# Reordering experts, attention pairs and the first pairs of a fused attention, expert and feed-forward kernel

## Chip, core and metric

One core of one Trainium2 chip runs the whole program in one launch. The metric is the device time of one execution in microseconds (us).

## What is computed

Inputs are `q`, `k`, `v` of shape (4, 8, 576, 64), embeddings of 8 experts with weights `w1` (8, 512, 1024) and `w2` (8, 1024, 512), and a feed-forward layer `w_in` (512, 2048), `w_out` (2048, 512).

```
q_rot, k_rot = rotate(q), rotate(k)
attn = softmax(scale * q_rot @ k_rot.T)            # per batch and head
x = (attn @ v) laid out as 2304 tokens x 512
idx = argmax over 8 experts of cosine(x, expert_emb) / tau;  gate = its softmax probability
y[token] = gate * relu(x @ w1[idx]) @ w2[idx]      # one expert for each token
h = y @ w_in;  g = h if h > 0 else exp(h) - 1
out = g @ w_out
```

With these inputs four experts get nearly all tokens: experts 1, 5, 6 and 2 get 709, 691, 722 and 173, experts 0 and 4 get 6 and 3, and two get none.

## The kernel before

**Attention.** The 32 heads run as 16 pairs p of two heads. A pair has nine score tiles. First come plain scores `sc` (PE, L327), whose row maxima `sc_max` (DVE, L337) are turned by `m_turn` (two PE matmuls, L347 and L348, a copy to fp16 on ACT, L350, and two small DMAs that ACT issues, L352 and L353) into a row of the stacked operand. Then come the scores again, less the maximum, `st` (PE, L363 and L364, exp on ACT, L365; no `st` tile of a pair may start before that row has landed). `p_lo` (L377, DVE or POOL) makes the low half of a split number, and `pv` (PE, L401) multiplies by v, followed by the row sums (L409). `o_out` (ACT) takes the result out, `o_turn` (PE, L427) transposes it, and `epi` (DVE, L442 to L451) divides by the sums. Operands of `sc` and `st` are made ahead: `load` (SP), `rope` (DVE or POOL), `hi` (ACT, L286) and `lo` (DVE, L290), and `stack`, six SP DMAs (L296 to L300) that copy the split halves into a buffer D4. Numbers are kept as a high and a low fp16 part, so most products take three matmuls.

**Routing and experts.** After each batch's four pairs `r_hi`, `r_lo`, `r_turn_pe`, `r_logits`, `r_acc` give logits, `r_pick`, `r_rank` and `r_slot` give every token a place, and `r_put` writes it out. The experts then run in visits j of up to 128 rows of one expert: visits 0 to 4 from the first three batches, before the last routing is known, and up to 20 more from tables (`tab_head`, `tab_visits`) that list experts in an order. In that order the early expert comes first, and then by size with small experts put between large ones. A visit is `mm1` (PE, L1057 to L1059), `relu` (L1069 ACT, L1070 DVE), `mm2` (PE, L1094 to L1096) and `y_out`. Where the expert changes (`chg`), `w_load` fetches its weights on SP as eight DMAs of 512 KB (L1009, L1012) and `w_conv` splits them (L1029 ACT, L1031 DVE); else a branch, `when` (L993), skips them. The tables give visits 0 to 5 to expert 1, 6 to expert 0, 7 to 12 to 5, 13 to 4, 14 to 19 to 6, and 20 and 21 to expert 2; three visits stay unused.

**Feed-forward.** Nine groups of 256 rows, `ff1` (L1139 to L1141), `elu`, `ff2` (L1191 to L1193), `fold`, store. Its weights are made into a form of 24 bits in two parts by `widen` on DVE, ACT and POOL during the earlier stages, column by column (32 columns), in weight buffers that `w_load` also uses: a buffer index b of 11 serves `w_load` until its column's due time.

**Order.** All tasks are listed with a hand-written time (`add(t, f, ...)`, corrected by the table OFF), sorted, and issued in that order to each engine's in-order queue. Pair p begins at 9p, the experts at ZV = 144.6; a visit is 2 units of ZU = 2.7.

Of the kernel before, what the change touches and what calls it, by code (L numbers as in the profile page):

```python
# [45 lines left out]
def kernel(ctx: ExitStack, tc: tile.TileContext, qk, vp, cs, cf, tid, emb, tau, w1, w2, wi, wo, out, tag=None):  # L46
# [174 lines left out]
    def emb_norm(i):  # L221
# [121 lines left out]
    def m_turn(p):  # L343
# [8 lines left out]
        nc.scalar.dma_start(out=d[64:65, 0, 1], in_=ms[0:5])  # L352
        nc.scalar.dma_start(out=d[0:1, 1, 1], in_=ms[5:10])  # L353
# [24 lines left out]

    def pv(p, kt):
# [309 lines left out]
    def tab_head():  # L689
# [113 lines left out]
    add(-22.0, c_prep)  # L803

    VT = (4.6, 6.2, 7.7, 9.6, 11.4)
    UT = [t - VT[0] for t in VT]
    for p in range(NP):
# [3 lines left out]
        add(z - 36 if p else z - 38.5, load, p, 1)  # L811
        for i in range(6):
            add(g - 33.3 + 1.5 * i if p else g - (33, 32.9, 32.85, 33, 32.8, 32.5)[i], rope, p, i)
        for f, i, t in ((hi, 0, -26.1), (lo, 0, -25), (hi, 1, -20.6), (lo, 1, -19.4)) if p else ((hi, 0, -25.6), (lo, 0, -24.6), (hi, 1, -24.5), (lo, 1, -23.6)):
            add(g + t, f, p, i)
        add(g - (19.3 if p else 23.5), stack, p)
        u, w = (z - 13.45, 1) if p else (z - 19, .3)
# [564 lines left out]
```

## Time and profile before

| | us |
|---|---|
| median of 3 runs | 1009.29 (1006.53 to 1009.57) |
| the profiled execution | 1010.61 |
| its span | 1008.8 |
| PE busy | 901.2 (89%) |
| DVE, POOL, ACT busy | 669.7, 546.3, 502.3 |
| PE idle before matmuls of L327 | 37.0 |

PE is the busiest engine and mostly full. What the span loses is idle time of PE in a few stretches and the time in which PE was granted half its clock (mean 0.948 of full). The stretches are the head (to 44 us), the 16 pairs (to 361), the passage from the last pair to the experts (to 385), the experts (to 631) and the feed-forward groups.

### The profile page before, as it was taken

How to read it: one execution, taken by the hardware profiler on the slowest of the kernel's cores; microseconds unless marked ns; L12 is line 12 of the kernel's file. 1: busy time of each engine (PE TensorE's matmuls, PEld its weight loads, DVE VectorE, ACT ScalarE, POOL GpSimd, SP SyncE). 2: the span in 40 equal slices, each digit the busy share in tenths (PEclk: the TensorE clock that was granted, in tenths of full speed). 3: DMA queues.
4: the chain of work that ended last, by engine and by line, in shares of the span. 5: the costliest groups of instructions: out<-in, count | busy, mean ns of one | idle time of the engine just before them, and what ended most of it. 6: DMA issues, size and time to landing. Idle time of an engine off the chain costs nothing. (4 is left out here: it accounts for less than half of the span.)

```text
span 1008.8 us, 24500 instructions
## 1 busy us (share of the span) xinstructions
PE 901.2 (89%) x9398; PEld 655.4 (65%) x9398; DVE 669.7 (66%) x1070; ACT 502.3 (50%) x858; POOL 546.3 (54%) x652
## 2 busy tenths in 40 slices
PE   3398999998989779999999876998999999999994
PEld 0154555554445467776776652887888888888884
DVE  8556757867868547778786874775665565664651
ACT  1244464464464633565665444645555555555540
POOL 6475565685643203424428544366776765766640
PEclk8588999999999979999999987999999999999998
DMA  7554465584463844997997674401201202201000
GB/s 261 152 166 107 129 156 136 142 200 127 133 144 104 251 85 144 328 249 200 260 304 175 192 203 92 123 2 43 64 22 43 64 22 43 65 22 44 22 22 21
DMA packets 127094, 127.65 MB, mean 127 GB/s; under 512 B 71272, under 2 KB 105064, under 8 KB 126960
## 3 DMA queue, kind: packets, MB, share of 16 engines
q1 hardware_dynamic: 118000, 97.68, 37.5%
q0 software_dynamic: 8352, 27.62, 8.5%
q8 instruction: 76, 1.25, 0.5%
q10 hardware_dynamic: 608, 0.63, 0.2%
q14 instruction: 58, 0.48, 0.2%
HBM read 79.15 MB, written 17.35 MB: 96 GB/s over the span
## 5 line engine op out<-in xcount | busy, mean ns | idle before, releaser
L1139 PE MATMUL banks<-arena 128*128 128x256 f16 x576 | 157.1, 273 | 2.4 <-ACT arena L1154 2.4
L1141 PE MATMUL banks<-arena 128*128 128x256 f16 x576 | 157.1, 273 | 0.0
L1140 PE MATMUL banks<-arena 128*128 128x256 f16 x576 | 157.1, 273 | 0.0
L365 ACT ACTIVATE arena<-banks 128x576 f32<-128x576 f32 x144 | 89.8, 652 | 125.8 <-PE banks L364 108.5
L1191 PE MATMUL banks<-arena 128*128 128x256 f16 x504 | 138.2, 274 | 5.5 <-DVE arena L1206 5.5
L1174 DVE TENSOR_TENSOR arena<-arena 128x896 f16<-128x896 f32 x72 | 79.9, 1110 | 89.0 <-ACT arena L1170 84.0
L1192 PE MATMUL banks<-arena 128*128 128x256 f16 x504 | 138.2, 274 | 0.0
L1193 PE MATMUL banks<-arena 128*128 128x256 f16 x504 | 138.2, 274 | 0.0
L1170 ACT ACTIVATE arena<-arena 128x896 f16<-128x896 f32 x71 | 67.5, 951 | 122.7 <-POOL arena L1167 121.4
L337 DVE TENSOR_REDUCE MH<-banks 128x1 f16<-128x576 f32 x144 | 103.2, 751 | 34.1 <-PE banks L327 32.3
L1059 PE MATMUL banks<-arena 128*128 128x128 f16 x704 | 122.4, 222 | 1.5 <-DVE arena L1031 1.5
L1057 PE MATMUL banks<-arena 128*128 128x128 f16 x704 | 122.5, 222 | 0.0
L1058 PE MATMUL banks<-arena 128*128 128x128 f16 x704 | 122.5, 222 | 0.0
L1164 POOL TENSOR_TENSOR arena<-arena 128x256 f32<-128x256 f32 x67 | 54.1, 808 | 91.4 <-DVE arena L1161 91.4
L983 POOL TENSOR_TENSOR arena<-arena 128x896 f16<-128x896 f32 (+1 forms) x32 | 51.6, 1611 | 86.1 <-ACT arena L981 65.7
L401 PE MATMUL banks<-arena 128*64 128x256 f32 (+9 forms) x768 | 90.9, 362 | 4.6 <-DVE arena L377 4.6
L363 PE MATMUL banks<-arena 128*128 128x288 f16 (+1 forms) x320 | 79.5, 299 | 3.5 <-DVE l L523 2.2
L327 PE MATMUL banks<-arena 64*128 64x288 f16 (+1 forms) x320 | 48.5, 313 | 37.0 <-DVE MH L337 16.2
L1095 PE MATMUL banks<-arena 128*128 128x512 f16 x176 | 70.2, 399 | 10.2 <-DVEq L993 9.6
L364 PE MATMUL banks<-arena 128*128 128x288 f16 (+1 forms) x320 | 78.5, 294 | 0.0
L1094 PE MATMUL banks<-arena 128*128 128x512 f16 x176 | 69.8, 396 | 6.0 <-ACT arena L1069 4.4
L377 POOL TENSOR_TENSOR arena<-arena 128x576 f16<-128x576 f32 x26 | 30.2, 1162 | 79.8 <-ACT arena L365 79.8
(238 smaller groups left out, 2285.2 us busy)
## 6 DMA issues: line engine op xcount, KB each, us to landing
arena<-in_w_dram SPq DMA_DIRECT2D x48, 512.0 KB
arena<-in_qk_dram SPq DMA_DIRECT2D x30, 576.0 KB
arena<-in_wo_dram SPq DMA_DIRECT2D x32, 256.0 KB
arena<-in_wi_dram SPq DMA_DIRECT2D x16, 512.0 KB
arena<-arena SPq DMA_DIRECT2D x32, 216.0 KB
yreg<-arena POOLq DMA_DIRECT2D x25, 260.0 KB, 4.0
arena<-arena SPq DMA_DIRECT2D x32, 144.0 KB
arena<-in_vp_dram SPq DMA_DIRECT2D x16, 256.0 KB
```

The source lines that it names most:

```text
L337: nc.vector.tensor_reduce(out=MH1[p % 2][:, c:c + 1], in_=t[:, :, 0:288], op=ALU.max, axis=AX.XY, negate=True)
L365: nc.scalar.activation(P32[:, (9 * p + i) % RP].rearrange("p (c n) -> p c n", c=2), t[:, :, 0:288], AF.Exp, scale=2.0)
L401: nc.tensor.matmul(o[64 * e:64 * e + 64, c, 0:QC[c].stop - QC[c].start], lhsT=w, rhs=x[:, QC[c]], start=first and n == 0, stop=end and n = ...
L1057: nc.tensor.matmul(o[:, fc], lhsT=w[:, 0, a], rhs=x[:, k], start=k == 0, stop=False)
L1058: nc.tensor.matmul(o[:, fc], lhsT=w[:, 0, a], rhs=x[:, 4 + k], start=False, stop=False)
L1059: nc.tensor.matmul(o[:, fc], lhsT=w[:, 1, a], rhs=x[:, k], start=False, stop=k == 3)
L1139: nc.tensor.matmul(o[:, v], lhsT=wih[k][:, f0:f0 + 128], rhs=z[:, :, k], start=k == 0, stop=False)
L1140: nc.tensor.matmul(o[:, v], lhsT=wih[k][:, f0:f0 + 128], rhs=z[:, :, 4 + k], start=False, stop=False)
L1141: nc.tensor.matmul(o[:, v], lhsT=wil[k][:, f0:f0 + 128], rhs=z[:, :, k], start=False, stop=k == 3)
L1191: nc.tensor.matmul(y, lhsT=a, rhs=b, start=u + f + n == 0, stop=False)
L1192: nc.tensor.matmul(y, lhsT=a, rhs=w[:, 1, WB[i - 1]], start=False, stop=False)
L1193: nc.tensor.matmul(y, lhsT=q[:, 1, f, GB[i - 1]], rhs=b, start=False, stop=u + f == 4 and n == len(m) - 1)
```

## The change

It has four parts. (1) **Head.** Pair 0's fourth rope goes from POOL to DVE; the 512-column cast of `c_prep` goes to ACT (`c_copy`), and the rest of `c_prep` later; `emb_norm` moves behind the first score tiles, with two operations from DVE to ACT; `warm` has 10 matmuls, not 13; `stack(0)` is issued half by SP and half by ACT, the pieces that `sc` reads first; pair 1's `hi`, `lo` and `stack` move to an own buffer and earlier; `sc(1)` moves from ahead of `st(0, 0)` to between the tiles of `st(0)`, and `sc(2)` later. (2) **Pairs.** The row sums become a task of their own, `ps`, 0.02 to 0.8 behind their `pv`; `m_turn` moves 0.78 later, and for p > 0 its DMAs go from ACT to SP; `o_out` moves 0.5 and `o_turn` 0.35 later. (3) **Passage.** `w_conv(0, ·)`: two in the middle of pair 15, two at its end; `p_lo`, `o_out`, `o_turn` of pair 15 earlier; its `r_turn_pe`, `r_logits` later, among the first visits' matmuls, as the tables. (4) **Experts.** The expert of rank 2 in the order gets 7 added, and so becomes the last: visits 14 and 15 go to expert 2, and 16 to 21 to expert 6; the `widen` columns 16 to 29 of `w_out` mostly move behind visit 17 (26 and 27 earlier), at 0.85 units a column in place of 0.9, so that four more weight buffers serve `w_load` until then.

```diff
+    def c_copy():
+        nc.scalar.copy(c16, cft[:, 0:512])
...
         elif i == 4:
-            nc.vector.tensor_scalar(et, et, n8[:, 1:2], 32.0, op0=ALU.mult, op1=ALU.mult)
+            nc.scalar.activation(et, et, AF.Copy, scale=n8[:, 1:2])
...
     def stack(p):
         h, t = hlt.pop(p), D4[p % 4]
+        if p == 0:
+            for e, eng in ((0, nc.sync), (1, nc.scalar)):
+                a, o = slice(64 * e, 64 * e + 64), slice(64 - 64 * e, 128 - 64 * e)
+                eng.dma_start(out=t[a, e, 0:3:2, 0:576], in_=h[a, 0:3:2])
+                eng.dma_start(out=t[a, e, 1, 0:576], in_=h[a, 1])
+                eng.dma_start(out=t[o, e, 0:3:2, 0:576], in_=h[a, 0:4:3])
+                eng.dma_start(out=t[a, e, 3, 0:576], in_=h[a, 2])
+            return
...
         d = D4[p % 4]
-        nc.scalar.dma_start(out=d[64:65, 0, 1], in_=ms[0:5])
-        nc.scalar.dma_start(out=d[0:1, 1, 1], in_=ms[5:10])
+        eng = nc.sync if p else nc.scalar
+        eng.dma_start(out=d[64:65, 0, 1], in_=ms[0:5])
+        eng.dma_start(out=d[0:1, 1, 1], in_=ms[5:10])
...
+        po[p, kt] = ones
+
+    def ps(p, kt):
+        o, ones, end = obank, po.pop((p, kt)), kt == PVO[-1]
...
+        pl_ = tbv(864, 8)
+        nc.vector.tensor_scalar(pl_, rk, 2.0, 7.0, op0=ALU.is_equal, op1=ALU.mult)
+        yield
         nc.vector.tensor_tensor(rk, rk, ps_, op=ALU.add)
+        yield
+        nc.vector.tensor_tensor(rk, rk, pl_, op=ALU.add)
...
-        add((-24.2, -24, -21.2, -21.1, -21, -20.9, -20.8)[i], emb_norm, i)
-    add(4, emb_turn)
-    add(-25.5, warm, OFF.get('WN', 13))
+        add((3.5, 5.5, 9.2, 9.3, 10.4, 11.4, 12.4)[i], emb_norm, i)
+    add(17.4, emb_turn)
+    add(-25.5, warm, 10)
...
-        u, w = (z - 13.45, 1) if p else (z - 19, .3)
+        ht = {0: (-25.6, -24.6, -24.5, -23.6, -23.5), 1: (-18.2, -18, -16.8, -16.5, -16.4), 2: (-8.2, -7, .4, .8, .9), 3: (4.8, 5.2, 6.4, 7.6, 7.7)}
...
+        u, w = {0: (-19, .3), 1: (.6, .6), 2: (6.2, .95)}.get(p, (z - 13.45, 1))
...
-        add(u + w * (UT[4] + (2.9 if p else 1.3)), m_turn, p)
+        add(u + w * (UT[4] + (3.68 if p else 1.3)), m_turn, p)
...
-                add(z + n + 1.8, p_lo, p, i)
-        for kt, t in zip(PVO, VT if p < NP - 1 else (4.6, 5.9, 7.5, 9.3, 10.4)):
+                add(z + n + (1.8 if p < NP - 1 else .9 if i < 8 else .4), p_lo, p, i)
+        for kt, t in zip(PVO, VT if p < NP - 1 else (4.6, 5.9, 7.5, 8.7, 9.4)):
             add(z + t, pv, p, kt)
-        add(z + (11.8 if p < NP - 1 else 10.6), o_out, p)
-        e = z + (14.7 if p < NP - 1 else 11.4)
+            add(z + t + (.01 if p == NP - 1 else ST5[kt]), ps, p, kt)
+        add(z + (12.3 if p < NP - 1 else 9.45), o_out, p)
+        e = z + (15.05 if p < NP - 1 else 10)
...
-            q, dt, sp = (y + 1, .2, .1) if last else (y + 10.2, .25, .5) if b == B - 2 else (y + 15.5, .5, 2.2)
+            q, dt, sp = (y + 6.8, .2, .1) if last else (y + 10.2, .25, .5) if b == B - 2 else (y + 15.5, .5, 2.2)
...
-    WT |= dict(zip(range(16, 30), (23.6, 30, 30.9, 31.8, 32.7, 33.6, 34.5, 35.4, 36.3, 37.2, 38, 39.3, 40.2, 42.2)))
+    WT |= dict(zip((26, 27, 16, 17, 18, 19, 20, 21, 22, 23, 24, 25, 28, 29), (23.2, 29, 34, 34.85, 35.7, 36.55, 37.4, 38.25, 39.1, 39.95, 40.8, 41.65, 42.5, 43.35)))
...
-            cv.append((use[j - 1, 2 * q + 1] + .01 if j else (-1.8, -1.1, -.4, .3)[q], j, q))
+            cv.append((use[j - 1, 2 * q + 1] + .01 if j else (-2.44, -1.85, .0075, .28)[q], j, q))
...
-        t0 = max(t0, free[b], {0: -4.8, 1: 0}.get(j, 1 if j < NE else 5.4)) + .001
+        t0 = max(t0, free[b], {0: -4.8, 1: 0}.get(j, 1 if j < NE else 5.8)) + .001
```

Line numbers shift: L290 becomes L293, L337 becomes L348, L350, L352 and L353 become L361, L364 and L365, L365 becomes L377, L1009 and L1012 become L1038 and L1041.

**DVE in the head.** The rows from the cast to the first maxima of pair 0 (L337 of before, L348 of after), before:

```order
L178 CAST c_67<-cft 128x512
L179 MEMSET tot 128x8
L180 RECIPROCAL rtau<-taut 128x1
L181 MEMSET chg 128x25
L182 TENSOR_SCALAR rtau<-rtau 128x1
L281 TENSOR_TENSOR arena<-arena 128x576
L227 TENSOR_SCALAR n_100<-n_100 8x1
L229 RECIPROCAL n_100<-n_100 8x1
L231 TENSOR_SCALAR arena<-arena,n_100 8x512
L233 CAST arena<-arena 8x512
L235 TENSOR_TENSOR arena<-arena 8x512
L337 TENSOR_REDUCE MH_92<-banks 128x1 x4
```

And after, from the third operation of the fourth rope (L284) on; L293 is `lo`:

```order
L284 TENSOR_TENSOR arena<-arena 128x576
L293 TENSOR_TENSOR arena<-arena 128x576 x2
L280 TENSOR_TENSOR arena<-arena 128x576
L284 TENSOR_TENSOR arena<-arena 128x576
L348 TENSOR_REDUCE MH_92<-banks 128x1 x4
L293 TENSOR_TENSOR arena<-arena 128x576
L348 TENSOR_REDUCE MH_92<-banks 128x1 x5
L352 COPY MH_94<-MH_92 128x1
```

The cast (L178), `c_prep` (L179 to L182) and `emb_norm` (L227 to L235) no longer stand ahead of the maxima; two rope operations (L280, L284) do.

**ACT in an ordinary pair.** From `o_out` of one pair (L415, L416) over exps (L365) and `m_turn` (L350 to L353) to `hi` (L286) and `r_hi` (L462), before:

```order
L415 COPY arena<-banks 128x384
L416 COPY arena<-banks 128x512
L365 ACTIVATE arena<-banks 128x576 x3
L350 CAST ms<-banks 10x128
L352 DMA arena<-ms 1x5x128
L353 DMA arena<-ms 1x5x128
L365 ACTIVATE arena<-banks 128x576
L286 ACTIVATE arena<-arena 128x576
L462 ACTIVATE arena<-arena 128x5x128
```

And after, where `o_out` is L433, the exp L377 and the copy of `m_turn` L361:

```order
L433 COPY arena<-banks 128x384
L434 COPY arena<-banks 128x512
L377 ACTIVATE arena<-banks 128x576 x3
L361 CAST ms<-banks 10x128
L289 ACTIVATE arena<-arena 128x576
L480 ACTIVATE arena<-arena 128x5x128
```

The two DMA issues have left ACT.

**SP in the passage.** From the reading of the first expert's number (`eidx`) over its weights, before:

```order
L1002 TENSOR_LOAD eidx
L1002 ISA x2
L1009 ISA
L1009 DMA arena<-in_w_dram 128x4x256
L1009 ISA
L1009 DMA arena<-in_w_dram 128x4x256
L1009 ISA
L1009 DMA arena<-in_w_dram 128x4x256
L1009 ISA
L1009 DMA arena<-in_w_dram 128x4x256
L1012 ISA
L1012 DMA arena<-in_w_dram 128x2x512
```

And after; L364 and L365 are `m_turn(15)`, which stood on ACT before:

```order
L1038 ISA
L1038 DMA arena<-in_w_dram 128x4x256
L1038 ISA
L1038 DMA arena<-in_w_dram 128x4x256
L1038 ISA
L1038 DMA arena<-in_w_dram 128x4x256
L1038 ISA
L1038 DMA arena<-in_w_dram 128x4x256
L364 DMA arena<-ms 1x5x128
L365 DMA arena<-ms 1x5x128
L1041 ISA
L1041 DMA arena<-in_w_dram 128x2x512
```

The last pair's two small DMAs now stand behind four weight loads in SP's queue and ahead of the other four.

## Rows read from the trace of the kernel before

**Rows 1.** waits of PE by what released them: us in total, times, longest.

```profile
PE banks L1095 <- DVEq L993: 9.6, 3, 4.0
...
PE banks L327 <- DVE arena L451: 7.0, 10, 0.7
PE banks L427 <- DVE MH L337: 6.5, 6, 2.0
```

**Rows 2.** windows: length; busy (x count) of PE, PEld, DVE, ACT, POOL; clock; DMA share, GB/s.

```profile
25.00:44.00 19.00, 5.06 (x23) 1.38 (x22) 10.10 (x18) 4.05 (x8) 5.60 (x5) 0.50 0.45 133
...
385.00:570.00 185.00, 185.00 (x2137) 136.35 (x2135) 142.26 (x201) 107.47 (x153) 81.36 (x108) 1.00 0.86 232
570.00:631.00 61.00, 43.42 (x306) 22.70 (x304) 40.35 (x61) 28.17 (x39) 27.53 (x36) 0.83 0.60 166
```

**Rows 3.** timeline of the head: start, us, engine, line, operation [idle before it, releaser].

```profile
11.51 1.40 SPq L296 DMA_DIRECT2D arena<-arena  x2
...
12.69 4.90 DVE L178 CAST c<-cft 128x512 f16<-128x512 f32 x1
...
15.79 0.29 PE L327 MATMUL banks<-arena 64*128 64x288 f16 x1 [2.01 <-DMA arena<-arena]
...
22.45 2.73 DVE L337 TENSOR_REDUCE MH<-banks 128x1 f16<-128x576 f32 x4
...
25.79 3.40 DVE L337 TENSOR_REDUCE MH<-banks 128x1 f16<-128x576 f32 x5
...
30.03 1.29 ACTq L352 DMA_DIRECT2D arena<-ms  x1
...
37.00 0.42 PE L327 MATMUL banks<-arena 64*128 64x288 f16 x1 [7.29 <-DMA arena<-arena]
...
44.09 0.40 PE L363 MATMUL banks<-arena 128*128 128x288 f16 x1
```

**Rows 4.** timeline of PE in pair 2, and the window behind it (PE alone).

```profile
93.40 1.09 PE L427 MATMUL banks<-cft,arena 128*128 128x128 f32 x8 [1.97 <-DVE MH L337]
94.00:100.00 6.00, 5.44 (x38) 0.57 0.29 74
```

**Rows 5.** timeline of the passage; the last line is a window of SP alone.

```profile
326.05 0.71 ACTq L352 DMA_DIRECT2D arena<-ms  x1
...
326.35 2.64 SPq L1009 DMA_DIRECT2D arena<-in_w_dram  x4
...
330.30 0.30 PE L363 MATMUL banks<-arena 128*128 128x288 f16 x1
...
354.07 1.39 PE L401 MATMUL banks<-arena 128*64 128x256 f16 x9 [3.97 <-DVE arena L377]
...
372.28 0.19 PE L570 MATMUL banks<-oh,c 128*128 128x40 f16 x1 [4.01 <-DVE oh L565]
...
330.00:332.00 2.00, 1.00 1.04 295
```

**Rows 6.** lines, 385 to 570 us (experts at pace): busy us, mean ns, idle before.

```profile
L1057 PE MATMUL banks<-arena 128*128 128x128 f16 x575 | 97.2, 219 | 0.0
...
L1095 PE MATMUL banks<-arena 128*128 128x512 f16 x138 | 52.4, 379 | 0.0
...
L1031 DVE SCALAR_TENSOR_TENSOR arena<-arena 128x1024 f16<-128x1024 f32 x32 | 38.5, 1233 | 5.8 <-ACT arena L1029 4.9 <-PE banks L1059 0.2
```

**Rows 7.** lines, 570 to 631 us (the experts end), and SP's timeline there.

```profile
L1095 PE MATMUL banks<-arena 128*128 128x512 f16 x32 | 15.5, 486 | 10.2 <-DVEq L993 9.6 <-DVE arena L1031 0.6
...
L1057 PE MATMUL banks<-arena 128*128 128x128 f16 x66 | 11.3, 219 | 0.0
...
L1029 ACT ACTIVATE arena<-arena 128x1024 f16<-128x1024 f32 x8 | 8.5, 1057 | 13.9 <-DMA arena<-in_w_dram 10.9 <-SPq L993 3.0
...
572.47 5.83 SPq L1009 DMA_DIRECT2D arena<-in_w_dram  x4
...
598.35 3.39 SPq L1012 DMA_DIRECT2D arena<-in_w_dram  x4
```

More of the change, by code (lines that the diff above doesn't have):

```diff
@@ L377, in p_lo @@
         eng.tensor_tensor(lo_slot(p, i), P32[:, r], PHB[:, r], op=ALU.subtract)
+    po = {}
     def pv(p, kt):
@@ L797 @@
     for i in range(7):
-        add((-24.2, -24, -21.2, -21.1, -21, -20.9, -20.8)[i], emb_norm, i)
-    add(4, emb_turn)
-    add(-25.5, warm, OFF.get('WN', 13))
+        add((3.5, 5.5, 9.2, 9.3, 10.4, 11.4, 12.4)[i], emb_norm, i)
+    add(17.4, emb_turn)
+    add(-25.5, warm, 10)
     for s, t in enumerate((-37, -36.9, -36.8, -36.7)):
         add(t, d_prep, s)
-    add(-22.0, c_prep)
+    add(-24.55, c_copy)
+    add(-10.1, c_prep)
     VT = (4.6, 6.2, 7.7, 9.6, 11.4)
     UT = [t - VT[0] for t in VT]
+    ST5 = (.7, .02, .5, .7, .8)
     for p in range(NP):
@@ L810 @@
         add(z - 39, load, p, 0)
-        add(z - 36 if p else z - 38.5, load, p, 1)
+        add({0: z - 38.5, 4: 1}.get(p, z - 36), load, p, 1)
         for i in range(6):
[L813 to L816, printed above, removed]
-        u, w = (z - 13.45, 1) if p else (z - 19, .3)
+            add((-23.3, -22.8, -21.3, -20.5, -19.3, -18.1)[i] if p == 1 else g - 33.3 + 1.5 * i if p else g - (33, 32.9, 32.85, 32.84, 32.8, 32.5)[i], rope, p, i)
+        ht = {0: (-25.6, -24.6, -24.5, -23.6, -23.5), 1: (-18.2, -18, -16.8, -16.5, -16.4), 2: (-8.2, -7, .4, .8, .9), 3: (4.8, 5.2, 6.4, 7.6, 7.7)}
+        ht = ht.get(p, tuple(g + t for t in (-26.04, -25, -20.54, -19.4, -19.3)))
+        for f, i, t in zip((hi, lo, hi, lo), (0, 0, 1, 1), ht):
+            tasks.append((t, len(tasks), f, (p, i)))
+        tasks.append((ht[4], len(tasks), stack, (p,)))
+        u, w = {0: (-19, .3), 1: (.6, .6), 2: (6.2, .95)}.get(p, (z - 13.45, 1))
         u += OFF.get(f'u@{p}', 0)
@@ L839 @@
             for g in range(5):
-                add(z - 34 + 3 * g + 6 * (b == 0), v_load, b, g)
+                add(-18.9 if b == 0 and g == 4 else z - 34 + 3 * g + 6 * (b == 0), v_load, b, g)
                 add(z - 25 + 3 * g + 6 * (b == 0), v_hi, b, g)
@@ L850 @@
                 add(y + 2.6 + d, r_turn_pe, p)
-                add(y + 4.5 + d, r_logits, p)
-                add(y + (5.6 if p < NP - 2 else 4.9) + d, r_acc, p)
+                add(y + (4.5 if p < NP - 2 else 3.15) + d, r_logits, p)
+                add(y + (5.6 if p < NP - 2 else 3.2) + d, r_acc, p)
         else:
             for i, f in enumerate((r_hi, r_lo, r_turn_pe, r_logits, r_acc)):
-                add(y + .1 * i, f, p)
+                add(y + (0, .1, 1.7, 5.5, 5.6)[i], f, p)
         if p == NP - 2:
             for t in range(5):
-                add(y + 2 + t, r_sq, b, 0, 0, 384, t)
+                add(y + 1.5 + .55 * t, r_sq, b, 0, 0, 384, t)
         if p % 4 == 3:
@@ L862 @@
                 for t in range(5):
-                    add(y + .25, r_sq, b, 1, 384, 512, t)
-                add(y + .35, r_sqsum, b)
-                add(y + .36, r_pow, b)
+                    add(y + 3.2, r_sq, b, 1, 384, 512, t)
+                add(y + 3.9, r_sqsum, b)
+                add(y + 4, r_pow, b)
             else:
@@ L887 @@
                 zt = q + dt * len(ops) + .1
-                steps(zt, .12, 21, tab_head)
+                steps(zt, .11, 23, tab_head)
                 steps(zt + 2.7, .1, 10, tab_visits)
@@ L1242, in addv @@
         add(ZV + ZU * a, f, *i)
-    wbuf, w1t, last = {}, {}, [-99, -99, -99, 5.2, -99]
+    wbuf, w1t, last = {}, {}, [-99, -99, -99, 6.3, -99]
     for c in sorted(range(32), key=wt):
@@ L1255 @@
             continue
-        n = min((0, 1, 2, 3) if c < 20 else (0, 1, 2) if c < 28 else (2, 4), key=lambda n: last[n])
+        n = min((0, 1, 2, 3) if t < 35 else (0, 1, 2) if c < 28 else (2, 4), key=lambda n: last[n])
         addv(max(t - OFF.get('WL', 3.3), (max(last[0], last[1], last[4]) if n == 4 else last[n]) + .01), widen_load, c // 16, c % 16)
```

12 lines of the change are left out of this document (6 added, 6 removed).

## The prediction

> **What bounds the kernel now.** I read the waits of PE first, then windows over the span, then the timelines of the stretches in which PE is not full. PE is busy 901 of 1008.8 us, and where it runs it runs at its pace: from 385 to 570 us it is busy 185.00 of 185.00 us at full clock [rows 2]. So a change of order can bring back only two things, PE's idle time and the time at half clock. They lie in four places. The head: the first `st` tile starts at 44.09, and PE's clock is at its lower level, 0.50 of full, from 25 to 44 [rows 2, 3]. The pairs: ten waits of `sc` on `epi`, 0.7 each, and three waits of `o_turn` that come to nearly all of 6.5 us [rows 1, 4]. The passage: two waits of 4 us [rows 5]. The experts' end: of 61 us from 570 to 631 PE is busy 43.4, with a clock of 0.83 [rows 2]. The reader is to see that the last is the largest.
>
> The sum is made against the profiled execution, 1010.61, which is 1.3 above the median of 1009.29; 1.3 comes off at the end.
>
> **Part 1, the head.** In before the first score tile waits for `stack(0)` to 15.79; its two first DMAs are issued in 1.40 from 11.51 [rows 3]. After, SP and ACT each issue one of the first pieces, so the tile starts some 0.7 earlier, at 15.1. The maxima then wait to 22.45, because the cast of 4.90 and `c_prep`, a rope product and `emb_norm` stand ahead on DVE [rows 3]. The order shows two short rope operations left there, so the first maximum follows the first tile at about 15.5. From first maximum to the issue of `m_turn`'s DMAs took 30.03 - 22.45 = 7.6, and nothing of it changes: 23.1. Their issue takes 2.0 in the head (1.29 and some 0.7), and a landing is bounded by 15.79 - 12.91 = 2.9, from the end of the issue of the stack's first two to the tile [rows 3]: 28.0. In before `sc(1)` stands between, which starts at 37.00 after 7.29 of waiting and is followed by `st(0)` at 44.09 [rows 3]. After, it lies among the `st(0)` tiles; its own PE work (20 matmuls, 2.8 of the 7.1 us from 37.00 to 44.09) is only moved. So st starts 16 earlier and owes 2.8: **-13**. Bounds: -16 if `sc(1)` hides fully; -8 if its operands are late again, since they still come through `hi(1)`, `lo(1)` and six DMAs, and a stall of some 5 of the old 7.29 opens inside `st(0)`. I take -13, since pair 1's ropes now go ahead of `v_hi`.
>
> **Part 2, the pairs.** Splitting off the row sums puts PE work behind `o_out`'s predecessors and costs no instruction. The `sc` that waited on `epi` [rows 1] now has other tiles ahead: 10 x 0.7 = 7.0, of which I leave 0.2 each for `o_out`, which stands an exp later: -5 (bounds 0 and -7). In pairs 2, 6 and 10 `o_turn` waits 1.97 for a maximum, and in the 6 us behind it PE is granted 0.57 [rows 4], which costs 6 x 0.43 = 2.6. Together 4.6 x 3 = 13.7. The maximum is late because DVE's `v_lo` waits for ACT's `v_hi`, which stands behind an exp; that stays. But `sc_max` runs ahead of `m_turn` by 0.78 units and `o_turn` comes 0.35 later, so I take two thirds: -9 (bounds 0 and -14). **-14** in all. The 30 DMA issues of `m_turn` leave ACT (0.71 each, [rows 5]), which is idle half the time: nothing. That they stand on SP from now on I price at 0 in the ordinary pairs, since 0.78 units later `m_turn` still lies 3 units (nearly 6 us) ahead of the first `st`, against some 1.4 of issue and 2.9 of landing; when that cover fails is the second rival.
>
> **Part 3, the passage.** The waits on `p_lo` (3.97) and `r_rank` (4.01) go [rows 5], since `p_lo` no longer stands behind `w_conv` on DVE and the tables stand behind the first visits' matmuls; some 2 us more of half clock behind each go too: -12. What is late next: `w_conv` takes DVE 2 x 1.23 [rows 6], and now two of them stand ahead of what turns pair 15's rows (`r_lo`), so PE meets a wait of up to 4.9 there; I take 4 and 1 of half clock: +5. And `m_turn(15)`: in before ACT issues at 326.05 and `st(15, 0)` starts at 330.30; SP issues four weight loads in 2.64 from 326.35, 2 MB, which at 295 GB/s [rows 5] are there by some 335. After, the two small DMAs are issued behind them. If they land with them, `st(15, 0)` is 4 to 5 late: +4. Sum **-3** (bounds -10, where neither comes, and +4).
>
> On this place the rows show that the DMA engines are full while the loads run (share 1.04, [rows 5]). The Trainium skill, "DMA: Bandwidth & Descriptors", section "Queues, rings and completion order", says that SP and ACT each own one row of rings, and that an engine takes turns between rows but drains one ring in order; by it, a small DMA on ACT's row passes the loads and one on SP's does not, which speaks against this move, here and in every pair. The section "Issuing engines are not separate DMA queues" of the same page says that issuing on another engine saves only sequencer time; by it alone the move would cost 2.6, and the part would be -5. No run here shows which.
>
> **Part 4, the experts.** At pace, 575 / 32 = 18.0 `mm1` visits and 138 / 8 = 17.25 `mm2` visits took 185 us, 10.5 a visit [rows 2, 6]. From 570 to 631 PE does 66 / 32 = 2.1 `mm1` and 32 / 8 = 4 `mm2` [rows 7], about 3.05 visits or 32 us: 61 - 32 = 29 too much. The cause stands in the rows: the weights of the change at visit 20 are issued from 572.47 to 601.74, and `w_conv` on ACT waits 10.9 for them, and 9.6 of PE's idle time is behind the branch of DVE's `w_conv` [rows 7]. They come so late because buffers have gone to the `widen` columns by then. After, the last change is at visit 16, some 42 us earlier, with four more buffers, and visits 17 to 21 keep their weights: no load, no split. I leave 5 of the 29: DVE and POOL now `widen` 12 columns at 0.85 units, denser than before, beside the reliefs of the last visits. **-24**. Bounds: -28, and -10 if the new change at 16 stalls, since 13, 14 and 16 need 12 MB within some 38 us on a core that moves 232 GB/s at pace [rows 2] (8.8 MB); the eleven buffers, 11 MB, hold most of it ahead, so I take the upper part.
>
> **Feed-forward.** It starts earlier by the sum and keeps its order; 0, bounds -3 and +3.
>
> Sum: -13 - 14 - 3 - 24 = -54: 1010.61 - 54 = 956.6, as a median **955**.
>
> **The rivals.** *The stall only moves:* the change at visit 16 waits for weights, or `widen` ends late and holds `ff1`; the tail gives 10, not 24: 969. For it: 12 MB in 38 us; against it: 11 buffers, and in before visits 13 and 14 change without a wait of PE. *The pairs give nothing:* `o_turn` waits on as before and its clock falls with it: 955 + 14 = 969. *The slower side:* `m_turn`'s DMAs on SP land late in every pair, behind `stack`'s six copies or a load. 15 pairs at t us each outweigh the rest (54) from t = 3.6. With a wait of 4 and 2.0 of half clock behind it 15 x 6 = 90: 955 + 90 = 1045. For it: the DMA engines have long full stretches; against it: `stack` of the next pair is issued behind `m_turn`. By the rule of the page above this is the case that would follow wherever a load stands ahead. *The change doesn't do what it says:* if the expert of rank 2 is not the large one, the weights still change at visit 20 and the tail stays: 955 + 24 = 979. The routing by the reference and the loads at 572.47 speak against it.
>
> **How the numbers follow.** The forecast (943 to 967) 0.60, the tail's stall moved 0.13, the pairs without gain 0.12, no effect on the tail 0.05, several of these at once (975 to 1005) 0.04, no change 0.02, slower 0.04. The range takes the forecast's bounds and the first three rivals: 936 to 981. Faster by over 0.3% 0.94, within 0.3% 0.02, slower 0.04; 0.3% is about what a measurement of this kernel can tell from no change.
>
> **What would show it.** Head: the first `st` near 28, no idle of PE over 4 before it. Pairs: no wait of L327's successor on `epi`; no window at 0.5 behind `o_turn`. Passage: no wait over 2 for `p_lo` and none for the ranks; the first `st` of pair 15 behind SP's loads. Tail: the last weight loads near 520 to 540 of the old time, PE full to `ff1`. I am wrong if `st` of ordinary pairs waits for a DMA, or if PE waits behind `w_conv` for visit 16.

## The result, and the profile after

The changed kernel takes 995.25 us (median of 4 runs, 991.61 to 1000.0) against 1007.92 for the kernel before on the same chip; the ratio is 0.987, with a 95% interval from 0.9844 to 0.9896. It is faster, by 13 us (1.3%) and not by 54, and lies outside the range of 936 to 981. The profiled execution took 994.5 with a span of 992.6, 16.2 less than the 1008.8 of before.

The table cuts the span at points that can be found in both traces. The measured column is the difference of the two profiled executions, in us; its sum is -16.2. The end of a product such as `mm2(17)` is taken at the start of its last matmul, here and below.

| stretch | before | after | measured | forecast |
|---|---|---|---|---|
| start to `st(2, 0)`: head and pairs 0, 1 | 81.9 | 71.1 | -10.8 | -13 |
| `st(2, 0)` to `st(15, 0)`: the pairs | 248.4 | 240.9 | -7.6 | -14 |
| `st(15, 0)` to `mm1(2, 0)`: the passage | 55.4 | 53.3 | -2.2 | -3 |
| `mm1(2, 0)` to the end of `mm2(17)`: experts at pace | 178.9 | 184.0 | +5.1 | 0 |
| end of `mm2(17)` to the first `ff2`: the experts' end | 97.1 | 97.0 | -0.1 | -24 |
| first `ff2` to the end | 347.0 | 346.4 | -0.6 | 0 |

So three terms came with the right sign and half to nearly all of their size, a new loss stands in the experts, and the largest term is not there at all. Single traces spread: in three more traces of the changed kernel the six stretches are 69.2 to 75.8, 239.8 to 246.0, 44.9 to 55.4, 182.0 to 186.9, 95.6 to 96.7 and 343.7 to 347.7. The signs of the first two and of the fourth hold in all of them, and the experts' end has lost next to nothing in any. Where PE waits in the kernel after, by what released it (us in total, times, longest):

```profile
PE banks L376 <- DMA arena<-ms: 10.7, 2, 6.2
PE banks L338 <- DVE MH L348: 10.1, 11, 3.6
PE banks L1123 <- ACTq L1022: 9.5, 2, 7.6
PE banks L1124 <- DVEq L1022: 6.1, 2, 3.2
...
PE banks L515 <- DVE arena L485: 4.2, 1, 4.2
...
PE banks L1168 <- ACT arena L1183: 3.5, 2, 3.1
```

The waits of `sc` on `epi` and of `o_turn` on a maximum [rows 1] are gone. New is the first line: `st` (L376) waits for the two small DMAs of `m_turn`, twice. The third and fourth line are the experts' end: `mm2` waits 15.6 there, hardly less than the 16.1 of its lines L1094 and L1095 before (10.2 of them in [rows 7]). The windows at the times of [rows 2], though the changed kernel is some 20 us further on in the second and third (length; busy and count of PE, PEld, DVE, ACT, POOL; clock; DMA share; GB/s):

```profile
25.00:44.00 19.00, 12.41 (x73) 4.84 (x73) 13.38 (x20) 8.19 (x15) 17.68 (x13) 0.58 0.76 228
385.00:570.00 185.00, 179.18 (x2031) 131.63 (x2030) 143.28 (x182) 105.82 (x151) 83.27 (x106) 0.99 0.97 251
570.00:631.00 61.00, 45.61 (x339) 29.71 (x337) 41.87 (x75) 28.89 (x47) 33.28 (x45) 0.86 0.43 117
```

The head has more than twice the PE work in the same window (12.41 against 5.06). In the second PE is no longer full, 179.18 of 185; about half of what it lacks lies behind 549.6, where `mm2(17)` has ended and the experts' end begins. The last window is nearly as empty as before: 45.61 of 61 against 43.42, with the clock at 0.86 against 0.83.

The head, PE's timeline (start, us, engine, line, [idle before]):

```profile
27.61 0.42 PE L376 MATMUL banks<-arena 128*128 128x288 f16 x1 [4.49 <-DMA arena<-ms]
33.94 0.40 PE L338 MATMUL banks<-arena 64*128 64x288 f16 x1 [3.58 <-DVE MH L348]
...
55.26 0.40 PE L375 MATMUL banks<-arena 128*128 128x288 f16 x1 [2.33 <-ACT arena L377]
```

and DVE's in the same place:

```profile
31.80 1.41 DVE L293 TENSOR_TENSOR arena<-arena 128x576 f16<-128x576 f32 x1 [0.46 <-ACT arena L289]
33.14 1.41 DVE L348 TENSOR_REDUCE MH<-banks 128x1 f16<-128x576 f32 x2
```

The first `st` can go on at 27.61, where `m_turn(0)`'s DMAs have landed; 28.0 was forecast. But then `sc(1)` waits 3.58 for its first maximum, which stands on DVE behind a `lo` of pair 2 (L293 at 31.80), and at 55.26 `st(1)` waits again. These two waits are among what the head gives back.

The passage, SP's timeline:

```profile
307.82 2.32 SPq L1038 DMA_DIRECT2D arena<-in_w_dram  x4
310.25 0.79 SPq L364 DMA_DIRECT2D arena<-ms  x1
311.09 0.66 SPq L365 DMA_DIRECT2D arena<-ms  x1
312.00 3.10 SPq L1041 DMA_DIRECT2D arena<-in_w_dram  x4
```

PE's timeline at `st(15, 0)`:

```profile
318.46 0.40 PE L376 MATMUL banks<-arena 128*128 128x288 f16 x1 [6.25 <-DMA arena<-ms]
```

and the window behind it (columns as above):

```profile
315.00:325.00 10.00, 6.54 (x52) 3.25 (x52) 0.00 (x0) 1.95 (x3) 1.66 (x2) 0.53 1.05 384
```

The two small DMAs (L364, L365) are issued right behind four weight loads, and the tile that needs them starts at 318.46, 6.7 after their issue ended. In the ten us from 315 PE has 0.53 of its clock while the DMA engines are full (share 1.05).

The experts' end, PE's timeline with its two longest waits:

```profile
595.80 0.59 PE L1123 MATMUL banks<-arena 128*128 128x512 f16 x1 [7.61 <-ACTq L1022]
599.58 0.59 PE L1124 MATMUL banks<-arena 128*128 128x512 f16 x1 [3.20 <-DVEq L1022]
```

ACT's timeline at the same time:

```profile
590.51 0.62 ACT L997 ACTIVATE arena<-arena 128x512 f32<-128x512 f32 x1
591.55 0.67 ACT L989 ACTIVATE arena<-arena 128x512 f32<-128x512 f32 x1 [0.43 <-DMA arena<-in_wo_dram]
594.27 0.95 ACT L1010 ACTIVATE arena<-arena 128x896 f16<-128x896 f32 x1 [2.04 <-POOL arena L1003]
595.12 0.58 ACT L1098 ACTIVATE arena<-banks 128x512 f16<-128x512 f32 x1
```

and the window:

```profile
590.00:605.00 15.00, 6.01 (x16) 2.14 (x17) 10.48 (x18) 7.06 (x11) 10.02 (x12) 0.54 0.25 71
```

`mm2(21)` needs `relu(21)` (L1098 on ACT, L1099 on DVE). Its `mm1` had ended at 580.5, yet ACT comes to the relu at 595.12, since steps of three `widen` columns (L997, L989, L1010) stand ahead, and the last of them waits 2.04 for POOL. No weight load is near: the last was issued at 522.19, 73 us earlier.

### The profile page after: what moved, and what is told of

Its sections match the earlier page's. It is cut to its first block, busy times and chain, and to the rows that moved or that the text cites. A ratio compares the mean times of both kernels' runs of the same rounds, so it can differ in the third digit from the quotient of the medians.

```text
span 992.6 us, 24586 instructions
## 1 busy us (share of the span) xinstructions
PE 894.5 (90%) x9395; PEld 652.4 (66%) x9395; DVE 669.0 (67%) x1073; ACT 505.1 (51%) x861; POOL 549.9 (55%) x649
## 5 line engine op out<-in xcount | busy, mean ns | idle before, releaser
L377 ACT ACTIVATE arena<-banks 128x576 f32<-128x576 f32 x144 | 93.3, 652 | 100.2 <-PE banks L376 94.7
L1220 PE MATMUL banks<-arena 128*128 128x256 f16 x504 | 138.2, 274 | 5.5 <-DVE arena L1235 5.5
L1222 PE MATMUL banks<-arena 128*128 128x256 f16 x504 | 138.2, 274 | 0.0
L1221 PE MATMUL banks<-arena 128*128 128x256 f16 x504 | 138.2, 274 | 0.0
L348 DVE TENSOR_REDUCE MH<-banks 128x1 f16<-128x576 f32 x144 | 103.0, 751 | 19.9 <-PE banks L338 19.8
L415 PE MATMUL banks<-arena 128*64 128x256 f32 (+9 forms) x768 | 92.5, 368 | 3.0 <-ACT arena L433 1.5
L376 PE MATMUL banks<-arena 128*128 128x288 f16 (+1 forms) x320 | 80.9, 299 | 10.7 <-DMA arena<-ms 10.7
L375 PE MATMUL banks<-arena 128*128 128x288 f16 (+1 forms) x320 | 81.8, 302 | 7.8 <-ACT arena L377 4.5
L1012 POOL TENSOR_TENSOR arena<-arena 128x896 f16<-128x896 f32 (+1 forms) x32 | 51.7, 1616 | 65.8 <-ACT arena L1010 51.9
L1123 PE MATMUL banks<-arena 128*128 128x512 f16 x176 | 67.8, 385 | 9.5 <-ACTq L1022 9.5
L1060 DVE SCALAR_TENSOR_TENSOR arena<-arena 128x1024 f16<-128x1024 f32 x48 | 58.7, 1263 | 24.7 <-ACT arena L1058 24.3
L1124 PE MATMUL banks<-arena 128*128 128x512 f16 x176 | 67.7, 385 | 6.1 <-DVEq L1022 6.1
L1086 PEld LDWEIGHTS <-arena 128*128 128x128 f16 x704 | 69.8, 99 | 4.1 <-ACTq L1022 1.9
```

What stands on the lines that cost most here:

```text
L348: nc.vector.tensor_reduce(out=MH1[p % 2][:, c:c + 1], in_=t[:, :, 0:288], op=ALU.max, axis=AX.XY, negate=True)
L377: nc.scalar.activation(P32[:, (9 * p + i) % RP].rearrange("p (c n) -> p c n", c=2), t[:, :, 0:288], AF.Exp, scale=2.0)
L1086: nc.tensor.matmul(o[:, fc], lhsT=w[:, 0, a], rhs=x[:, k], start=k == 0, stop=False)
L1220: nc.tensor.matmul(y, lhsT=a, rhs=b, start=u + f + n == 0, stop=False)
L1221: nc.tensor.matmul(y, lhsT=a, rhs=w[:, 1, WB[i - 1]], start=False, stop=False)
L1222: nc.tensor.matmul(y, lhsT=q[:, 1, f, GB[i - 1]], rhs=b, start=False, stop=u + f == 4 and n == len(m) - 1)
```

## The experiments

A variant is set against runs of before on its own chip. Chips differ (before took 1008 to 1018, after/before 0.974 to 0.988), so ratios are compared on one chip only, and lengths of stretches across all. Two lengths recur, in us; they are taken from each run's trace, A from the end of `mm2(4)` to the end of `mm2(17)`, B from there to the first `ff2`:

| kernel | order of experts | widen times | A | B | A + B |
|---|---|---|---|---|---|
| before | old | old | 137.0 | 97.1 | 234.2 |
| order_only | new | old | 144.4 | 83.2 | 227.6 |
| order_undone | old | new | 137.0 | 104.6 | 241.6 |
| after (four runs) | new | new | 137.0 to 138.2 | 95.6 to 97.0 | 233.0 to 235.2 |
| widen_old | new | old | 143.7 | 81.3 | 225.0 |
| widen_slow | new | 1.2 apart | 137.8 | 95.9 | 233.7 |
| widen_cut | new | cut | 137.0 | 76.6 | 213.6 |
| no_branch | new | new | 137.0 | 93.8 | 230.8 |
| combo, best3, best2 | new | old | 142.9 to 147.1 | 81.4 to 84.1 | 225.8, 228.5, 230.5 |

### Is the experts' end held by the weights or by the widen columns?

**order_undone** takes the new order out of the changed kernel:

```diff
-        nc.vector.tensor_scalar(pl_, rk, 2.0, 7.0, op0=ALU.is_equal, op1=ALU.mult)
+        nc.vector.tensor_scalar(pl_, rk, 2.0, 0.0, op0=ALU.is_equal, op1=ALU.mult)
```

> The changed kernel with the 7 added to rank 2 replaced by 0: the order of experts is that of before (last change of weights at visit 20), all times as in the changed kernel. My prediction (the tail is held by the late weight loads of visit 20): 24 us more, about 1019. Theory T (the tail is held by the widen columns, which run late on DVE, ACT and POOL in either order, and the relu steps stand behind them): 0 to 6 us more, 995 to 1001.

Its one time was 1011.51, between the 995 to 1001 of theory T and the 1019 of my prediction; the changed kernel on the same chip (after_same) took 988.21 to 998.68. Against the trace of after_same its span is 12.9 longer, of which 4.3 stand ahead of `mm2(4)`, where the order has not yet played a part (it concerns visits 14 on), and 8.6 in A + B. A + B is 241.6, 6.4 to 8.6 more than in the four runs of after; theory T allowed 6, my prediction 24. The waits of PE from 550 to 640 us in its trace:

```profile
PE banks L1123 <- ACTq L1022: 8.4, 1, 8.4
PE banks L1124 <- DVEq L1022: 6.7, 2, 3.5
PE banks L1123 <- ACT arena L1058: 2.5, 1, 2.5
PE banks L1124 <- DVE arena L1060: 1.5, 1, 1.5
```

The splits of visit 20's weights (L1058, L1060) cost PE 4.0; the 15.1 ahead of them is there with either order.

**order_only** is the other way round, the kernel before with the order alone:

```diff
+        nc.vector.tensor_scalar(pl_, rk, 2.0, 7.0, op0=ALU.is_equal, op1=ALU.mult)
...
+        nc.vector.tensor_tensor(rk, rk, pl_, op=ALU.add)
```

> The kernel before with nothing but the new order of experts (7 added to rank 2; last change of weights at visit 16). My prediction: 24 us less than before. Theory T (the order is worth only the loads and splits of one change, 7 us by the run with the order undone): 5 to 10 us less than before, since its widen columns start earlier but are as late at the end.

It took 1014.3 in its one run, where before has a median of 1017.5. The time falls by less than A + B, since `mm1(5)`, ahead of A, now waits 5.29 for its rows. A + B is 6.6 less than before: B falls by 13.9 and A grows by 7.4, since at visit 16, the new place of the change, PE now waits for the splits of the weights (L1034 on ACT, L1036 on DVE), 4.9 in all with one wait behind their branch, and is granted 0.89 of its clock from 560 to 575:

```profile
560.62 0.38 PE L1100 MATMUL banks<-arena 128*128 128x512 f16 x1 [0.79 <-DVE arena L1036]
...
564.67 0.38 PE L1099 MATMUL banks<-arena 128*128 128x512 f16 x1 [1.41 <-ACT arena L1034]
...
566.77 0.58 PE L1100 MATMUL banks<-arena 128*128 128x512 f16 x1 [1.72 <-DVE arena L1036]
```

So the loads of visit 20 were worth 13.9 of the experts' end, and half of that came back at visit 16. In sum the order is worth 6.4 to 8.6 us, in both directions.

**widen_cut** leaves most of the widening of 12 columns out (the first lines of the edit):

```diff
+        if w == 1 and c < 14 and c not in (10, 11):
+            n = slice(0, 8)
+            a4, d4, t4 = a.rearrange("p (a b) -> p a b", a=4)[:, :, n], t[:, 0:4, n], tf[:, :, n]
...
```

> The changed kernel with the widening of the 12 late columns of w_out cut to 8 of every 128 elements in all five steps, and ff2 reading one finished column block throughout (part of the computation is left out). Theory T (late widen steps hold the relus): the stretch from the end of mm2(17) to the first ff1 falls from 62 to 38 to 42 us, 20 to 24 us less. If the tail is held by something else (weights, gathers, branches alone): less than 5 us.

From the end of `mm2(17)` to the first `ff1` it needs 42.1 where after has 60.7, 18.6 less, a little short of the 20 to 24 expected, and B is 20.4 less. PE's waits from 540 to 650 us:

```profile
PE banks L1197 <- ACT arena L1212: 3.4, 1, 3.4
PE banks L1153 <- DVEq L1051: 1.6, 1, 1.6
PE banks L1152 <- ACTq L1051: 1.1, 1, 1.1
```

The waits of `mm2` fall from 15.6 to 2.7 with no change to weights or order. B of the changed kernel spreads over 1.4 in four traces, so one trace settles it: with the new order and the new times, the late columns hold the experts' end.

**no_branch** asks whether the branches around weights that are never loaded make the columns late:

```diff
+        if 17 <= j <= 21:
+            return
         ch = nc.values_load(chg[0:1, j:j + 1], engines=engines, min_val=0, max_val=1)
```

> The changed kernel with the conditional weight loads and splits of visits 17 to 21 left out of the program (with these inputs they are never taken, so the result is the same): 20 branches fewer on DVE, on ACT and on SP. If the branches (some 0.9 us each on DVE, not counted as busy) are what makes the widen columns late: the stretch from the end of mm2(17) to the first ff1 falls from 62 to 47 to 54 us, 8 to 15 us less. If they are not: 0 to 3 us less.

B is 93.8, 1.8 to 3.2 less than in the four runs of after, as was expected if they don't matter. They cost a little and are not the cause. (One run, 991.67.)

### Does a wider pitch help?

**widen_slow**:

```diff
-(23.2, 29, 34, 34.85, 35.7, ..., 43.35)
+(23.2, 29, 34.00, 35.20, 36.40, ..., 47.20)
```

> The changed kernel with the 12 late columns of w_out spaced 1.2 units apart in place of 0.85 (6.3 us, the pitch at which they really ran, in place of 4.5), starting at the same time. Theory T (relu steps of the last visits stand behind widen steps that run late): the relus come on time, the stretch from the end of mm2(17) to the first ff2 falls from 97 to 80 to 88 us, 9 to 17 us less. If the engines are simply too busy in that stretch (theory L, load and not order): the wait only moves to ff2, 0 to 4 us less.

The relus came on time but for one (`mm2` still waits 4.94 at 591.21), and B did not move: 95.9 against 95.6 of after on the same chip; the ratio to before is 0.9791 (0.9762 to 0.9821) against 0.9739 (0.9698 to 0.978). The time from `mm2(17)` to `ff1` fell by 11.9, but the waits moved on to the feed-forward stage, as PE's timeline there shows:

```profile
614.02 0.27 PE L1168 MATMUL banks<-arena 128*128 128x256 f16 x1 [2.63 <-DVEq L1022]
...
626.46 0.37 PE L1168 MATMUL banks<-arena 128*128 128x256 f16 x1 [7.99 <-ACT arena L1183]
...
638.17 0.27 PE L1168 MATMUL banks<-arena 128*128 128x256 f16 x1 [1.18 <-ACT arena L1183]
```

B stayed, as theory L had it: the columns end late all the same, and what is put behind them waits. Its reason, that the engines are too busy, does not fit: from 528 to 608 in after DVE is busy 51.7 of 80, POOL 50.4 and ACT 34.7. The columns run at 6.7 us each there: 12 in the 80 us, as the count of one of their DVE steps shows, where 0.85 units are 4.5.

```profile
L1012 POOL TENSOR_TENSOR arena<-arena 128x896 f16<-128x896 f32 x10 | 19.0, 1903 | 19.0 <-ACT arena L1010 15.1 <-ACTq L1022 3.9
...
L1010 ACT ACTIVATE arena<-arena 128x896 f16<-128x896 f32 x11 | 10.4, 949 | 26.9 <-POOL arena L1003 8.8 <-DVEq L1022 6.4 <-POOL arena L1132 5.6
...
L994 DVE SCALAR_TENSOR_TENSOR arena<-arena 128x512 uint32<-128x512 uint32 x12 | 10.0, 832 | 0.4
```

The last two columns of these rows (idle before, and for whom) point to why: POOL stands 19.0 before its step, 15.1 of it for ACT, and ACT 26.9 before its own, 14.4 of it for POOL. That this waiting for one another sets the pitch is read from these rows and was not tested; what the least pitch of this chain would be with more work buffers was not tried either.

**widen_old** puts the columns back to their times in the kernel before (columns 7 to 15 too, which the change had moved by up to 0.4 units; the edit is cut):

```diff
-    WT |= dict(zip((26, 27, 16, 17, ...), (23.2, 29, 34, 34.85, ...)))
+    WT |= dict(zip(range(16, 30), (23.6, 30, 30.9, 31.8, ...)))
...
-        n = min((0, 1, 2, 3) if t < 35 else (0, 1, 2) if c < 28 else (2, 4), key=lambda n: last[n])
+        n = min((0, 1, 2, 3) if c < 20 else (0, 1, 2) if c < 28 else (2, 4), key=lambda n: last[n])
```

> The changed kernel with the times of the widen columns of before (columns 16 to 29 from 23.6 to 42.2 at 0.9 units), the new order of experts kept. Theory T and L together (the columns are bound by the three engines' throughput, so starting later only ends later): from the end of mm2(4) to the first ff2 235 becomes 226 to 229 us, 6 to 9 us less. My prediction's reason for the move (buffers for the loads of the change at visit 16): without them the loads of visit 16 stall and it is 0 to 10 us more.

A + B is 225.0, 8.1 less than the 233.1 of after on the same chip; 989.13 (983.19 to 994.07) against 994.81 (991.2 to 998.16); the two intervals of the ratio overlap. The loads of visit 16 do cost: A is 6.7 longer. B gives 14.8 back. combo, best2 and best3 below have the same order and the same columns, and their A + B is 3.5 to 7.3 less than in after on their chips. So the new widen times, taken alone, cost 3.5 to 8 us, about what the new order had gained.

### m_turn(15) on SP

**ms15_act**:

```diff
-        eng = nc.sync if p else nc.scalar
+        eng = nc.sync if 0 < p < NP - 1 else nc.scalar
```

> The changed kernel with one line different: the two small DMAs of m_turn(15) are issued by ACT again, those of pairs 1 to 14 stay on SP. Theory A (they wait in SP's queue behind 2 MB of weight loads): the wait of 6.2 us before st(15, 0) goes, and of the half clock behind it some 3 us, so 9 us less, about 986. Theory B (the DMA engines are full there and a small DMA is late on either queue): 0 to 2 us less, the wait of L376 on a DMA stays near 6.

The wait of L376 on a DMA is gone, though the DMA engines are full (share 1.03 from 310 to 315), which speaks against theory B; PE's waits from 300 to 345 us are now

```profile
PE banks L415 <- ACT arena L433: 1.8, 1, 1.8
PE banks L415 <- ACT arena L434: 1.7, 1, 1.7
PE banks L415 <- issue: 1.3, 1, 1.3
PE banks L515 <- ACT arena L377: 1.2, 1, 1.2
```

In the eleven runs with these DMAs on SP the wait was 0.2, 1.5, 1.7, 1.8, 2.1, 2.1, 6.2, 7.7, 8.3, 8.5 and 8.6; in the four with them on ACT there was none. The Trainium skill, "DMA: Bandwidth & Descriptors", section "Queues, rings and completion order", says that SP and ACT each own one row of rings and that on each engine descriptors are consumed in ring order. These runs agree.

The 9 us of theory A didn't come in this run. Its ratio to before, 0.9775 (0.9738 to 0.9812), is no better than that of after_same on the same chip, 0.9739 (0.9698 to 0.978), and from `st(2, 0)` to `mm1(2, 0)` it needs 293.9, where the four runs of after need 290.9 to 295.9. The traces show why. Some 10 us ahead of `st(15, 0)`, `pv` (L415) is held for 2 to 3 us, mostly by `o_out` (L434), here and in six of the eleven runs with the DMAs on SP. In these six `st(15, 0)` waits 0.2 to 2.1, in the five others 6.2 to 8.6. after_same is one of the six; its waits from 300 to 332 us are

```profile
PE banks L415 <- ACT arena L434: 1.7, 1, 1.7
...
PE banks L415 <- issue: 1.2, 1, 1.2
...
PE banks L376 <- DMA arena<-ms: 0.2, 1, 0.2
```

What brings this hold about was not settled. widen_old and best2 (below) differ in the line of ms15_act alone, though not on one chip, and have no such hold: from `st(2, 0)` to `mm1(2, 0)` they need 294.6 and 286.9. There the move to ACT is worth 7.7 us, near the 9 of theory A.

### The head

**headfix** moves pair 2's second half behind the first maxima of `sc(1)` (pair 2's entry in the table `ht`):

```diff
-2: (-8.2, -7, .4, .8, .9)
+2: (-8.2, -7, 2.2, 3.3, 3.4)
```

> The changed kernel with hi, lo and stack of pair 2's second half 1.8 to 2.5 units later, so that DVE's lo(2, 1), which waits for POOL's rope, no longer stands ahead of the maxima of sc(1). If that place is what pair 0 loses: the wait of 3.6 us in sc(1, 1) goes and st(2, 0) comes 3 to 4 us earlier. If another late operand takes its place (stack(2) for sc(2), or hi(4) on ACT): 0 to 1 us.

In this kernel `load(4, 1)` has overwritten what `hi(2, 1)` reads, so pair 2's values and with them the routing change; only its head can be read. The wait in `sc(1)` was 2.11; it did not go, and eleven traces with the head of after have 1.5 to 4.3 there. The next wait was 2.36 in `sc(2)`, and none stood ahead of `st(1, 1)`. `st(2, 0)` came at 70.3, where the four runs of after have 69.2 to 75.8. So a gain isn't shown.

**hi4_late** moves a step of pair 4 on ACT (an entry added to `ht`):

```diff
-3: (4.8, 5.2, 6.4, 7.6, 7.7)}
+3: (4.8, 5.2, 6.4, 7.6, 7.7), 4: (11.6, 12.2, 15.46, 16.6, 16.7)}
```

> The changed kernel with hi(4, 0) on ACT 1.6 units later, behind the exp of st(1, 4) and of st(1, 1). If ACT's in-order queue behind hi(4, 0), which waits for the buffer that stack(3) reads, is what holds st(1, 1): its wait of 2.3 to 7.5 us goes and st(2, 0) comes by as much earlier. If st(1, 1) waits for something else: no change, 0 to 1 us.

The theory fell. The wait of L375 went, and others took its place, as PE's timeline shows:

```profile
34.31 0.40 PE L338 MATMUL banks<-arena 64*128 64x288 f16 x1 [4.79 <-DVE MH L348]
...
49.74 0.22 PE L359 MATMUL banks<-c,MH 128*10 128x128 f16 x1 [2.37 <-DVE MH L352]
...
64.64 0.64 PE L338 MATMUL banks<-arena 64*128 64x288 f16 x3 [2.34 <-DVE MH L348]
```

`o_turn(0)` came at 70.5, where the four runs of after have 61.8, 63.6, 68.1 and 68.3. That spread of 6.5 within one kernel is the wait ahead of `st(1, 1)`: 1.33, 2.33, 7.79 and 7.46 in the same order. Of the eleven traces with this head five wait 6.9 to 7.8 there and have `o_turn(0)` at 68.0 to 68.6; in the other six it comes at 61.8 to 65.6. What decides it stays open.

### The change with two parts undone

**combo** joins ms15_act, hi4_late and widen_old; **best2** leaves hi4_late out; **best3** adds headfix, with `load(4, 1)` moved too:

```diff
-            add({0: z - 38.5, 4: 1}.get(p, z - 36), load, p, 1)
+            add({0: z - 38.5, 4: 3.45}.get(p, z - 36), load, p, 1)
```

> The three single edits together: m_turn(15) on ACT, hi(4, 0) later, widen columns at their old times. If they are independent: 7 for the columns, 2 to 7 for hi(4, 0), 0 to 6 for m_turn(15), so 9 to 18 us less than the changed kernel on the same chip. If the gain is given back at the first ff2: under 5 us.

> The changed kernel with two parts of the change undone: m_turn(15)'s DMAs on ACT and the widen columns at their old times. If the two are independent and the edit of hi(4, 0) in the combination cost time: 12 to 20 us less than the changed kernel, 975 to 983. If the combination's 12 us were all: 10 to 13 less.

> The same and, in the head, hi, lo and stack of pair 2's second half 1.8 to 2.5 units later, with load(4, 1), which reuses their buffer, 2.45 later. If lo(2, 1) ahead of sc(1)'s maxima on DVE is what the head loses: the wait of 2 to 4 us in sc(1, 1) goes and nothing as long comes, 2 to 4 us less than the kernel with two parts undone. If the next late operand takes its place: within 1 us, or more.

The changed kernel ran beside them on each chip, as after_same, after_again and after_third:

> The changed kernel itself once more, so that the variants of this call have it on the same chip. Ratio to before 0.975 to 0.990; st(15, 0) waits 1 to 7 us for the DMAs of m_turn(15); from the end of mm2(17) to the first ff2 97 us.

> The changed kernel itself, as the measure for the variants of this call on its chip. Ratio to before 0.970 to 0.990.

> The changed kernel itself, as the measure on this chip. Ratio to before 0.970 to 0.990.

| kernel | median, us | ratio to before (95%) | after on the same chip |
|---|---|---|---|
| combo | 982.50 (976.92 to 984.45) | 0.9739 (0.9700 to 0.9778) | 994.81, 0.9878 (0.9849 to 0.9908) |
| best2 | 981.03 (976.96 to 986.69) | 0.9711 (0.9667 to 0.9755) | 994.80, 0.9853 (0.9816 to 0.9891) |
| best3 | 976.59 (975.70 to 980.48) | 0.9677 (0.9642 to 0.9713) | 994.80, 0.9853 (0.9816 to 0.9891) |

after_same was at 993.46, 0.9739 (0.9698 to 0.978), a little below the 0.975 to 0.990 expected, on the chip where before is slowest. combo brings 12.3 us and best2, with two parts undone, 13.8, both in the range expected. best3 is 4.4 lower still, a little more than expected, but the two intervals overlap, and the trace of best2 is one of the five with the long wait ahead of `st(1, 1)`; what the fix of the head is worth is not shown. best3 beats both kernels, by 33 us before and 18 us after. The first lines of PE's waits in it:

```profile
PE banks L317 <- ACT arena L289: 9.2, 1, 9.2
PE banks L338 <- DVE MH L348: 8.3, 11, 1.7
PE banks L1124 <- DVEq L1022: 5.5, 2, 2.9
PE banks L1220 <- DVE arena L1235: 5.5, 2, 3.6
```

No wait of the experts' end is over 2.9 any more, and `st(15, 0)` waits for no DMA.

## Why the prediction was wrong

**The head** (-13 forecast, -10.8 measured). The chain to the first `st` was right step by step: maxima at 15.50 (15.5 forecast), the DMAs done at 27.61 (28.0). The step that was too good is the last, that `sc(1)` only owes its 2.8: `sc(1)` waited 3.58 (2.0 to 2.6 in the other three runs of after). The bound "its operands are late again" had a stall there, but for pair 1's operands; the trace has a `lo` of pair 2 ahead of the maxima on DVE, and with that moved away headfix still waits 2.11. And the wait ahead of `st(1, 1)`, 1.3 to 7.8, was not in the sum. In the four runs of after the stretch fell by 6.1 to 12.6, so that -10.8 is near the forecast in part by luck.

**The pairs** (-14, -7.6). The waits on `epi` went as forecast. The mis-sized term is the "two thirds of 13.7", 9, for pairs 2, 6 and 10: their steps to the next pair gave 4.2 (2.3 and 2.8 less, and 0.9 more for pair 6). All waits of PE over 0.25 between `st(2, 0)` and `st(15, 0)` come to 19.9 before and 16.2 after. Two dips of the clock stay, 0.62 to 0.69 from 145 to 155 and 0.66 from 290 to 295. In most pairs small new waits of 0.6 to 1.1 on maxima and exps stand where the 0.7 on `epi` was.

**The passage** (-3, -2.2). Right in sum, and both parts larger: `m_turn(15)` cost 6.25 where +4 was forecast (7.7 with what follows it, by best2 against widen_old), and the rest, from the tile at 318.46 on, gained 8.7 where -7 was. That they cancel as forecast is partly luck: the stretch is 44.9 to 55.4 in the four runs of after. The wait on `r_lo` behind `w_conv` was 4.16, forecast 4.

**The experts at pace** (0, +5.1). Not forecast: `mm1(5)` waits 1.73 for its transposed rows and then meets 0.69 of the clock; 1.0 more at visit 16. The tables now come later and SP issues weight loads between its transposes, but that this is the cause is not shown: order_only, whose tables stand at their old times with two more steps, waits 5.29 in the same place.

**The experts' end** (-24, -0.1). Here the prediction failed, at the sentence "The cause stands in the rows", which puts all 29 us on the weights of visit 20, and at the 5 left for the columns. The waits for weights were real, but two things were late behind the same matmuls. Taking the loads away at the old column times shortens B by 13.9, not by 29, and 7.4 came back as the stall at visit 16, which the prediction had as a bound. The four buffers do end that stall: A is 137 to 138 with them. But to free them the columns moved back, and that lengthens B by 12.6 to 15.3 (after against widen_old, combo, best2 and best3, each on its chip), where 5 was left for "denser than before". The two moves cancel. In before too the columns ran late, some 10 us at 570 and, against visits at their full pace, 30 at 612, worked out from the start of a column's last step against its place between the visits. [rows 2] show DVE busy 142 of 185 us at pace, but a column that crosses three in-order queues five times did not run at the busiest engine's share. The rival of the moved stall named both mechanisms, the change at visit 16 and a late `widen`, with 0.13, and still left 10 of the 24.

**The slower side** fell as stated: no `st` of pairs 1 to 14 waits for SP. It held for the one pair with a load ahead.

## What to carry to other kernels

Before a wait is removed, ask who else is late at that point, and from whom the cure takes its buffers: here two things were late behind the same matmuls, and the buffers that cured one delayed the other. Work that passes between several in-order queues has a pitch of its own, and it is read from the distance of its last steps in the trace, not from the sum of busy times; moving such work later costs what it ends later, unless what it frees is worth more. A small DMA that something waits for shouldn't share a queue with bulk loads.

## What the runs showed of the hardware

Two DMAs of 1.2 KB each, issued behind 2 MB of loads on one queue, made their reader wait between 0.2 and 8.6 us in eleven runs, and not once in four on the other queue; the longer waits, 6.2 to 8.6, came where PE reached the reader without an earlier hold. The 128x512 cast that took 4.90 us on DVE beside POOL's work took 0.62 on ACT. One head, in eleven traces, brought its first pair to `o_turn` between 61.8 and 68.6 us.

```profile
10.51 0.62 ACT L178 CAST c<-cft 128x512 f16<-128x512 f32 x1 [1.64 <-DMA cft<-in_cf_dram]
```
